# Spreading out the passage between the attention and the first expert stage: ten units of expert 0, one group's token sums, the Sinkhorn steps

## The chip, the cores and the metric

The kernel runs on one core of one Trainium2 chip. The engines of that core work at the same time, each through its own queue in order: TensorE (PE in the profile, with PEld for its weight loads), VectorE (DVE), ScalarE (ACT), GpSimd (POOL) and SyncE (SP, which here only issues transfers). The metric is the device time of one launch in microseconds (us), lower is better.

## What is computed

```python
# attention: r, k, v are [4, 8, 768, 48]; w, u are [8, 48]
for t in range(S):
    cur = einsum('bhd,bhe->bhde', u * k[t], v[t])
    y[t] = einsum('bhd,bhde->bhe', r[t], state + cur)
    state = w * state + einsum('bhd,bhe->bhde', k[t], v[t])
x = y.transpose(0, 2, 1, 3).reshape(3072, 384)
# eight experts over all 3072 tokens, with a Sinkhorn gate
P = exp(x @ w_gate - max)                  # [3072, 8]
for _ in range(8):
    P /= P.sum(1, keepdims=True) + 1e-09   # over the experts
    P /= P.sum(0, keepdims=True) + 1e-09   # over the tokens
    P *= N / E
out = sum over e of P[:, e:e+1] * (relu(x @ w1[e]) @ w2[e])   # w1 [8, 384, 1024], w2 [8, 1024, 384]
```

## The kernel before

**Attention.** The 3072 tokens are 24 tiles of 128. A loop over `i` (0 to 26) carries each tile through stages `prep`, `stage_b` to `stage_f`, one tile per pass and each stage one or more passes behind the one before it. At its end a tile stands in `hbx` as x transposed, in two float16 parts (high, and what is left), and its gate logits in `logits`. Three tiles make a position `po_` (384 tokens); there are eight.

**Expert 0** is computed plainly, in *units*. `g1_unit(po_, fc, W)` forms 128 hidden columns of one position: nine products of 128x384 into the PSUM tile `ph` (pool `ps1`, two banks), then a relu on ACT into `hb` (high part) and a scalar_tensor_tensor on DVE (low part, which needs the high one). `g2_half(po_, t, j, W)` is half of the second layer for one tile: twelve products into `po` (pool `ps2`, two banks), a copy on ACT into `stg`, and a store to `e0d` in DRAM by the SP queue. 109 units are made; `run` places three of them in each pass of the attention from `i` = 5 on, which leaves 43 units and the last three halves of the second layer (`pend`).

**Experts 1 to 7** are 14 stages of half an expert. Their first layer uses a scheme with 15 products in place of 18: the 384 inputs of a half's weights are combined into 15 weight sums, the tokens into 15 token sums. The token sums come in four groups `sg` of 768 tokens: `combine_tokens` gives `rebuild` (three DVE additions of the two parts of x), `singles` (four copies by transfers on the SP queue), `pool` (17 additions on POOL), and `high` and `low` in four pieces (`PARTS`): a cast on ACT and a difference on DVE into `xv`. Groups 0 and 1 (into `xv0`) are made in the attention, one step at each call of `prepare`; groups 2 and 3 (into `xv1`) after it. `stage_weights` does the like for weights: `load` into `rawb`, four `amax` on DVE, the maximum over the partitions (`reduce_max`, `across`, `scale`: two tiny products on PE with DVE work between them), 11 additions on POOL into `ucb`, eight pieces of `high` (ACT) and `low` (DVE) into `ws0` or `ws1`.

**The tick loop** lies between the attention and stage 0, and its order is written out by hand. Each tick does what `at(t, ...)` lists for it and then issues one unit of expert 0. It holds group 2, the first stage's weights `W0`, group 3, and the Sinkhorn: a generator `sk` of 21 steps, of which 16 are half steps (`rs` is the half over experts, on DVE alone; `cs` the half over tokens, a product `pc` on PE and then DVE). From tick 4 on a half step stands at every second tick, to tick 36.

**Stage s** is a row of *slots*. `g1_slots(s, g, j)` gives 15 slots of three products 128x512 each (tiles `bA`, `bY`, `bZ`, `bC`, `bB`, with DVE and ACT sums after most slots); `g` is the half of the tokens, `j` the half of the columns. Between the slots 24 products per five slots are taken from `rest`: in the first half of stage 0 (`g` = 0, 30 slots) that is `e0_rest`, the 36 products of `pend`; from then on it is `g2_tiles`, 144 products for the second layer of the group before. The stage's `at(t, ...)` puts weight work of the next stage at slots. A bank for a first-layer tile is taken from `ps4` (four banks), every third one from `ps1`. `gate()` and `gate0()` form the weights by which the second layer's results are scaled, from the finished gate `pm`.

All instructions carry line 29, where a helper records them; so they are told apart by their tiles.

Of the kernel before, what the change touches and what calls it, by code (L numbers as in the profile page):

```python
# [32 lines left out]
def rwkv_sinkhorn_moe(  # L33
# [175 lines left out]
    def g1_unit(po_, fc, W):  # L209
        w1h, w1l = W[0], W[1]  # L210
        hh, hl = h0(fc // FHC)
        ph = ps1.tile([P, TB], F32, tag="ph", name=f"ph_{po_}_{fc}")[:, :TB0]
        fs = slice(fc * P, (fc + 1) * P)
        for c in range(KC):
            xh_, xl_ = xx8[:, po_, c], xx8[:, po_, KC + c]
            T.matmul(ph, w1h[:, c, fs], xh_, start=(c == 0), stop=False)
            T.matmul(ph, w1h[:, c, fs], xl_, start=False, stop=False)
            T.matmul(ph, w1l[:, c, fs], xh_, start=False, stop=(c == KC - 1))
        fl = fc % FHC
        S_.activation(hh[:, fl, :], ph, AF.Relu)  # L220
        V.scalar_tensor_tensor(
            hl[:, fl, :], ph, 0.0, hh[:, fl, :], op0=ALU.max, op1=ALU.subtract
        )
# [450 lines left out]
    def token_steps(sg, *homes):  # L674

        rebuild, singles, pool, high, low = combine_tokens(sg, *homes)
        steps = [[lambda th=th: rebuild(th)] for th in range(TH)]
        steps[-1].append(singles)
        steps += [[f] for f in pool] + [[], [], [], []]
# [14 lines left out]
    def run(n, ready=True):  # L694
        prepare()
        if not ready:
            spin(5)
            return
        for _ in range(n):
            if units:  # L700
                units.pop(0)()

    W, side = split_weights(0, *raws, ws1)
    for sg in range(2):
        steps = token_steps(sg, ws0, 0, ws0, 9 * TS)
        need[id(steps[0])] = (sg + 1) * 2 * TH
        side += steps
# [4 lines left out]
    for i in range(NTT + 3):  # L712
# [28 lines left out]
        if 3 <= i < 8:  # L741
            prepare()
# [3 lines left out]
        if 0 <= done < NTT and done % TH == TH - 1:  # L746
            po_ = done // TH
            for j in range(2):
                g1 = [lambda fc=fc, po_=po_: g1_unit(po_, fc, W) for fc in range(j * FHC, (j + 1) * FHC)]
                g2 = [lambda a=a: whole(g2_half(*a, W)) for a in pend]  # L750
# [137 lines left out]
    WS = {0: stage_weights(0)}  # L888
    sk = sinkhorn()
    at(0, WS[0]["load"])  # L890
    for j in range(4):
        at(j, lambda: next(sk, None))
    for j in range(8):
        at(4 * j + 4, lambda: next(sk, None))
        at(4 * j + 6, lambda: next(sk, None))
    at(36, lambda: next(sk, None))

    def plan_tokens(sg, t_build, t_pool, pool_rate, t_parts, homes):
        rebuild, singles, pool, high, low = combine_tokens(sg, *homes)
        for th, t in enumerate(t_build):  # L900
            at(t, lambda th=th: rebuild(th))
        at(t_build[-1], singles)
        for i, f in enumerate(pool):
            at(t_pool + i // pool_rate, f)
        for (i, n), t in zip(((0, 3), (3, 3), (6, 3), (9, 4)), t_parts):
# [3 lines left out]
    plan_tokens(2, (0, 1, 2), 3, 3, (5, 7, 8, 10), (ucb, 0, tb_, 0))  # L909
    W0 = WS[0]  # L910
    for i, t in enumerate((4, 5, 9, 10)):
        at(t, lambda i=i: W0["amax"](i))
    at(11, W0["reduce_max"])
    at(12, W0["across"])
    for i, f in enumerate(W0["pool"]):
        at(9 + i // 3, f)
    at(14, W0["scale"])
    for n, i in enumerate((0, 1, 2, 3, 4, 5, 6, 7)):
        at(15 + n, lambda i=i: W0["high"](i))
        at(16 + n, lambda i=i: W0["low"](i))  # L920
    plan_tokens(3, (20, 20, 21), 21, 3, (24, 26, 27, 29), (ucb, 0, tb_, 0))

    tick = 0
    while units or any(t >= tick for t in ticks):
        for f in ticks.pop(tick, []):
            f()
        if units:
            units.pop(0)()
# [12 lines left out]
    def bank(name):  # L941
        n = chains[0]
        chains[0] += 1
        if n % 3 == 2:
# [152 lines left out]
    def stage_tasks(s):  # L1097
# [8 lines left out]
        at(2, gate)  # L1106
        if s == 0:
            at(3, gate0)
# [28 lines left out]
    def e0_rest():  # L1137
        for a_ in pend:
# [50 lines left out]
```

## Time and profile before

| | |
|---|---|
| three timed runs | 1598.94 us median (1598.56 to 1601.12) |
| the profiled execution, its own time | 1598.68 us |
| its span, first to last instruction | 1597.0 us |
| PE busy | 1567.8 us, 98% of the span |
| DVE, ACT, POOL busy | 1021.9, 668.0, 586.6 us |

Times in views are counted from the span's start. In a timeline row stand the start, the length, the engine, the line, the operation with its tiles, how many instructions the row merges, and in brackets the idle time of the engine ahead of it with what ended it. A row of the view by windows gives, for one stretch, its length, then busy time and instructions of PE, PEld, DVE, ACT and POOL, the granted PE clock as a share, the share of the transfer engines and GB/s. In the chain of work that ended last the rows are start, length, engine and tile; a product's length there is the time until the next one, without its drain, and so gives PE's rate.

### The profile page before, as it was taken

Reading aid. Unit: us, or ns where it says so; the run is one execution under the profiler, and the core shown is the slowest. Engines: PE = TensorE matmul, PEld = TensorE weight load, DVE = VectorE, ACT = ScalarE, POOL = GpSimd, SP = SyncE. Lnnn points to the kernel's source line nnn. Section 1 sums busy time; section 2 is a strip of 40 time slices with the busy share of each in tenths; the row PEclk is TensorE's granted clock in tenths of the full one; section 3 lists DMA queues with packets and bytes.
Section 4 is the critical chain, followed back from the end, with each engine's and each line's share of the span. In section 5 each row is a group of like instructions: output and inputs, shape, how many; then the busy total and the mean of one; then the engine's idle time right before and its main releaser. Section 6 shows DMA issues by size and latency. Waiting matters only on the chain.

```text
span 1597.0 us, 24269 instructions
## 1 busy us (share of the span) xinstructions
PE 1567.8 (98%) x9394; PEld 907.6 (57%) x9394; DVE 1021.9 (64%) x1693; ACT 668.0 (42%) x1190; POOL 586.6 (37%) x688
## 2 busy tenths in 40 slices
PE   7999999989999999999999999999999999999999
PEld 4777777655455555555555555555555555555555
DVE  6766766675766676666667666666666666656554
ACT  2333333343444444454535454544444453535420
POOL 6557665452020342424242424243242424242200
PEclk9999999999999999999999999999999999999999
DMA  7323330212122566666665666665555555555443
GB/s 179 64 65 77 78 87 26 89 44 84 34 95 58 104 88 115 88 124 87 122 95 86 113 88 120 89 115 62 94 58 95 60 97 59 95 59 89 60 93 129
DMA packets 167643, 138.32 MB, mean 87 GB/s; under 512 B 90337, under 2 KB 161762, under 8 KB 167522
## 3 DMA queue, kind: packets, MB, share of 16 engines
q0 software_dynamic: 44928, 61.36, 31.9%
q1 hardware_dynamic: 122384, 75.35, 16.9%
q8 instruction: 75, 1.23, 0.3%
q14 instruction: 46, 0.38, 0.1%
q10 hardware_dynamic: 210, 0.00, 0.0%
HBM read 55.39 MB, written 80.23 MB: 85 GB/s over the span
## 4 chain that ended last, share of the span: by engine, by line
PE 93%; DVE 3%; POOL 1%; issue 1%; ACT 1%; DMA 0%; ACTq 0%; DVEq 0%; POOLq 0%
PE po L29 46%; PE bY L29 11%; PE bZ L29 11%; PE ph L29 5%; PE bA L29 4%; PE bB L29 4%; PE py L29 4%; PE bC L29 2%; PE pA L29 1%; PE pu L29 1%; POOL tb L29 1%; PE prT L29 1%; PE pz L29 1%; PE pkT L29 1%; PE px L29 0%
## 5 line engine op out<-in xcount | busy, mean ns | idle before, releaser
L29 PE MATMUL po<-ws,hbx 128*128 128x384 f16 x3360 | 737.3, 327 | 0.0
L29 POOL DMA_DIRECT2D accd<-stg x288 | 249.8, 867 | 695.4 <-ACT stg L29 675.5
L29 PEld LDWEIGHTS <-hbx 128*128 128x128 f16 x3576 | 338.0, 98 | 291.4
L29 PEld LDWEIGHTS <-ws 128*128 128x128 f16 x3096 | 303.1, 98 | 251.9 <-issue 10.2
L29 ACT ACTIVATE hbx<-tb 128x512 f16<-128x512 f32 x224 | 141.0, 630 | 445.6 <-DVE tb L29 445.6
L29 PE MATMUL po<-ws,hb 128*128 128x384 f16 x1248 | 323.4, 328 | 3.2 <-DVE ws L29 2.3
L29 DVE TENSOR_TENSOR tb<-bY,tb 128x512 f32<-128x512 f32 x168 | 116.1, 691 | 195.3 <-PE bY L29 195.1
L29 ACT ACTIVATE stg<-po,pe 128x384 f32<-128x384 f32 x312 | 179.1, 574 | 121.8 <-PE po L29 94.9
L29 PE MATMUL bZ<-xv,ws 128*128 128x512 f16 x840 | 227.8, 381 | 1.4 <-DVE tb L29 1.4
L29 PE MATMUL bY<-xv,ws 128*128 128x512 f16 x840 | 227.8, 381 | 1.1 <-DVE tb L29 1.1
L29 DVE TENSOR_TENSOR tb<-bZ,tb 128x512 f32<-128x512 f32 x168 | 115.4, 687 | 134.2 <-PE bZ L29 134.2
L29 PEld LDWEIGHTS <-hb 128*128 128x128 f16 x1248 | 122.1, 98 | 96.5 <-issue 5.0
L29 POOL TENSOR_TENSOR ucb<-rawb 128x256 f32<-128x256 f32 x84 | 75.0, 943 | 94.8 <-DMA rawb<-in_moe_w_dram 68.3
L29 DVE TENSOR_TENSOR tb<-bB,tb 128x512 f32<-128x512 f32 x112 | 77.4, 691 | 48.9 <-PE bB L29 47.0
L29 PE MATMUL ph<-hbx,ws 128*128 128x384 f16 x576 | 103.8, 329 | 1.2 <-DVE hb L29 1.2
L29 DVE SCALAR_TENSOR_TENSOR hb<-tb,hbx 128x512 f16<-128x512 f32 x112 | 77.3, 690 | 24.6 <-ACT hbx L29 19.5
L29 PE MATMUL bA<-xv,ws 128*128 128x512 f16 x336 | 90.9, 380 | 1.0 <-ACT tb L29 1.0
L29 PE MATMUL bB<-xv,ws 128*128 128x512 f16 x336 | 90.9, 380 | 0.0
L29 DVE SCALAR_TENSOR_TENSOR hbx<-tb,hbx 128x512 f16<-128x512 f32 x112 | 78.2, 698 | 14.7 <-ACT hbx L29 10.4
L29 DVE SCALAR_TENSOR_TENSOR hb<-ph,hb 128x384 f16<-128x384 f32 x64 | 35.5, 555 | 58.9 <-ACT hb L29 58.8
L29 ACT COPY tb<-bZ 128x512 f32<-128x512 f32 x56 | 32.8, 585 | 67.6 <-PE bZ L29 67.6
L29 ACT ACTIVATE hb<-ph 128x384 f16<-128x384 f32 x64 | 31.4, 491 | 58.0 <-PE ph L29 56.7
(165 smaller groups left out, 1638.3 us busy)
## 6 DMA issues: line engine op xcount, KB each, us to landing
accd<-stg POOLq DMA_DIRECT2D x288, 192.0 KB, 3.7
rawb<-in_moe_w_dram SPq DMA_DIRECT2D x28, 768.0 KB, 7.3
e0d<-stg SPq DMA_DIRECT2D x48, 192.0 KB, 1.9
hb<-e0d SPq DMA_DIRECT2D x48, 192.0 KB, 3.7
rn<-in_r_dram SPq DMA_DIRECT2D x24, 192.0 KB, 3.1
kn<-in_k_dram SPq DMA_DIRECT2D x24, 192.0 KB, 3.6
vn<-in_v_dram SPq DMA_DIRECT2D x24, 192.0 KB, 2.7
accd<-stg SPq DMA_DIRECT2D x24, 192.0 KB, 1.8
```

Source lines behind the costliest of these rows:

```text
L29: return lambda *a, **k: self.tc.keep_in_program_order(f(*a, **k))
```

## The change

Five things, all between the last passes of the attention and the end of the first half of stage 0.

1. Expert 0's last ten units (six `g1_unit`, four `g2_half`) are taken off the tick loop, which keeps 33. They go ahead of `pend` in `e0_rest`, so that 138 products (102 and 36) are there for the 144 places between the 30 slots. For this `g1_unit` becomes a generator that stops after each product.
2. Group 2's `rebuild` and its 17 POOL additions become steps of the attention (`token_steps(..., sums=True)`), in `ws0` and not in `ucb` and `tb`. `prepare` is called once or twice more in a pass from `i` = 21. Its casts and differences stay in the tick loop, at ticks 0 to 7, its `singles` go from tick 2 to 0.
3. Group 3 comes ahead of the weights: `rebuild` at ticks 0 to 2, `singles` at 2, casts at 8 to 14 (before: 20 and 21, 21, 24 to 29). `W0`'s `across` and `scale` go from ticks 12 and 14 to 14 and 17, its `high` and `low` from 15 to 23 to 18 to 26.
4. The Sinkhorn's half steps stand two or three ticks apart (4, 7, 9, 12, ... 32), and the last five steps at slots 2, 5, 9, 13 and 18 of stage 0. `gate` and `gate0` of that stage move from slots 2 and 3 to 24 and 25.
5. The first ten banks of the first layer all come from `ps4`, since `ph` of the moved units uses `ps1`.

```diff
@@ -207,6 +207,7 @@
         return (part(hb3, F16, 2 * j * n, (FHC, TB0)), part(hb3, F16, (2 * j + 1) * n, (FHC, TB0)))
 
     def g1_unit(po_, fc, W):
+
         w1h, w1l = W[0], W[1]
         hh, hl = h0(fc // FHC)
         ph = ps1.tile([P, TB], F32, tag="ph", name=f"ph_{po_}_{fc}")[:, :TB0]
@@ -214,13 +215,17 @@
         for c in range(KC):
             xh_, xl_ = xx8[:, po_, c], xx8[:, po_, KC + c]
             T.matmul(ph, w1h[:, c, fs], xh_, start=(c == 0), stop=False)
+            yield
             T.matmul(ph, w1h[:, c, fs], xl_, start=False, stop=False)
+            yield
             T.matmul(ph, w1l[:, c, fs], xh_, start=False, stop=(c == KC - 1))
-        fl = fc % FHC
-        S_.activation(hh[:, fl, :], ph, AF.Relu)
-        V.scalar_tensor_tensor(
-            hl[:, fl, :], ph, 0.0, hh[:, fl, :], op0=ALU.max, op1=ALU.subtract
-        )
+            if c == KC - 1:
+                fl = fc % FHC
+                S_.activation(hh[:, fl, :], ph, AF.Relu)
+                V.scalar_tensor_tensor(
+                    hl[:, fl, :], ph, 0.0, hh[:, fl, :], op0=ALU.max, op1=ALU.subtract
+                )
+            yield
 
     def g2_half(po_, t, j, W):
 
@@ -671,12 +676,15 @@
 
     PARTS = ((0, 3), (3, 3), (6, 3), (9, 4))
 
-    def token_steps(sg, *homes):
-
-        rebuild, singles, pool, high, low = combine_tokens(sg, *homes)
+    def token_steps(parts, sums=False):
+
+        rebuild, singles, pool, high, low = parts
         steps = [[lambda th=th: rebuild(th)] for th in range(TH)]
-        steps[-1].append(singles)
-        steps += [[f] for f in pool] + [[], [], [], []]
+        steps += [[f] for f in pool]
+        if sums:
+            return [lambda fs=fs: [f() for f in fs] for fs in steps]
+        steps[2].append(singles)
+        steps += [[], [], [], []]
         for (i, n), at_ in zip(PARTS, (5, 11, 15, 19)):
             steps[TH + at_].append(lambda i=i, n=n: high(i, n))
             steps[TH + at_ + 1].append(lambda i=i, n=n: low(i, n))
@@ -698,11 +706,12 @@
             return
         for _ in range(n):
             if units:
-                units.pop(0)()
+                whole(units.pop(0))
 
     W, side = split_weights(0, *raws, ws1)
-    for sg in range(2):
-        steps = token_steps(sg, ws0, 0, ws0, 9 * TS)
+    early = [combine_tokens(sg, ws0, 0, ws0, 9 * TS) for sg in range(3)]
+    for sg in range(3):
+        steps = token_steps(early[sg], sg == 2)
         need[id(steps[0])] = (sg + 1) * 2 * TH
         side += steps
     prep(0)
@@ -738,7 +747,9 @@
         if 1 <= i <= NTT:
             stage_d(i - 1)
         prepare()
-        if 3 <= i < 8:
+        if 3 <= i < 8 or i >= 21:
+            prepare()
+        if i >= 22:
             prepare()
         if 3 <= i:
             stage_f(i - 3)
@@ -746,8 +757,8 @@
         if 0 <= done < NTT and done % TH == TH - 1:
             po_ = done // TH
             for j in range(2):
-                g1 = [lambda fc=fc, po_=po_: g1_unit(po_, fc, W) for fc in range(j * FHC, (j + 1) * FHC)]
-                g2 = [lambda a=a: whole(g2_half(*a, W)) for a in pend]
+                g1 = [g1_unit(po_, fc, W) for fc in range(j * FHC, (j + 1) * FHC)]
+                g2 = [g2_half(*a, W) for a in pend]
                 units += merged(g1, g2)
                 pend = [(po_, t, j) for t in range(TH)]
     assert not side
@@ -885,47 +896,49 @@
     def at(t, *fs):
         ticks.setdefault(t, []).extend(fs)
 
-    WS = {0: stage_weights(0)}
-    sk = sinkhorn()
-    at(0, WS[0]["load"])
-    for j in range(4):
-        at(j, lambda: next(sk, None))
-    for j in range(8):
-        at(4 * j + 4, lambda: next(sk, None))
-        at(4 * j + 6, lambda: next(sk, None))
-    at(36, lambda: next(sk, None))
-
-    def plan_tokens(sg, t_build, t_pool, pool_rate, t_parts, homes):
-        rebuild, singles, pool, high, low = combine_tokens(sg, *homes)
-        for th, t in enumerate(t_build):
-            at(t, lambda th=th: rebuild(th))
-        at(t_build[-1], singles)
-        for i, f in enumerate(pool):
-            at(t_pool + i // pool_rate, f)
-        for (i, n), t in zip(((0, 3), (3, 3), (6, 3), (9, 4)), t_parts):
+    def at_parts(high, low, t_parts):
+        for (i, n), t in zip(PARTS, t_parts):
             at(t, lambda i=i, n=n: high(i, n))
             at(t + 1, lambda i=i, n=n: low(i, n))
 
-    plan_tokens(2, (0, 1, 2), 3, 3, (5, 7, 8, 10), (ucb, 0, tb_, 0))
-    W0 = WS[0]
-    for i, t in enumerate((4, 5, 9, 10)):
+    W0 = stage_weights(0)
+    WS = {0: W0}
+    sk = sinkhorn()
+    at(0, W0["load"])
+    for t in (0, 1, 2, 3, 4, 7, 9, 12, 14, 17, 19, 22, 24, 27, 29, 32):
+        at(t, lambda: next(sk, None))
+
+    _, singles2, _, high2, low2 = early[2]
+    at(0, singles2)
+    at_parts(high2, low2, (0, 2, 4, 6))
+
+    rebuild3, singles3, pool3, high3, low3 = combine_tokens(3, ucb, 0, tb_, 0)
+    for th in range(TH):
+        at(th, lambda th=th: rebuild3(th))
+    at(2, singles3)
+    for i, f in enumerate(pool3):
+        at(2 + i // 2, f)
+    at_parts(high3, low3, (8, 10, 12, 14))
+
+    for i, t in enumerate((5, 8, 9, 11)):
         at(t, lambda i=i: W0["amax"](i))
     at(11, W0["reduce_max"])
-    at(12, W0["across"])
+    at(14, W0["across"])
     for i, f in enumerate(W0["pool"]):
-        at(9 + i // 3, f)
-    at(14, W0["scale"])
-    for n, i in enumerate((0, 1, 2, 3, 4, 5, 6, 7)):
-        at(15 + n, lambda i=i: W0["high"](i))
-        at(16 + n, lambda i=i: W0["low"](i))
-    plan_tokens(3, (20, 20, 21), 21, 3, (24, 26, 27, 29), (ucb, 0, tb_, 0))
-
+        at(11 + i // 2, f)
+    at(17, W0["scale"])
+    for i in range(W0["n"]):
+        at(18 + i, lambda i=i: W0["high"](i))
+        at(19 + i, lambda i=i: W0["low"](i))
+
+    e0_last = units[-10:]
+    del units[-10:]
     tick = 0
     while units or any(t >= tick for t in ticks):
         for f in ticks.pop(tick, []):
             f()
         if units:
-            units.pop(0)()
+            whole(units.pop(0))
         tick += 1
 
 
@@ -941,7 +954,7 @@
     def bank(name):
         n = chains[0]
         chains[0] += 1
-        if n % 3 == 2:
+        if n % 3 == 2 and n >= 10:
             return ps1.tile([P, TB], F32, tag="ph", name=name)
         return ps4.tile([P, TB], F32, tag="pq", name=name)
 
@@ -1103,9 +1116,11 @@
         def gate():
             pes[s] = gate_of(1 + s // 2, WS[s]["isw"], s)
 
-        at(2, gate)
+        at(2 if s else 24, gate)
         if s == 0:
-            at(3, gate0)
+            at(25, gate0)
+            for t in (2, 5, 9, 13, 18):
+                at(t, lambda: next(sk, None))
         if s + 1 < NS:
             w_ = WS[s + 1] = stage_weights(s + 1)
             at(0, w_["load"])
@@ -1135,6 +1150,8 @@
         return ts
 
     def e0_rest():
+        for u_ in e0_last:
+            yield from u_
         for a_ in pend:
             yield from g2_half(*a_, W)
 
```

Three places show what moves. The first is **POOL at the end of the attention**: `rk` is the attention's last work there, `tb<-ucb` are token sums after it, `ws_74` is `ws0`. Before:

```order
L29 TENSOR_TENSOR rk_6445<-rk_6445,hbx 128x384
L29 TENSOR_TENSOR S_6625<-S_6625,wbd 128x384
L29 TENSOR_TENSOR rk_6571<-vn_6187,dg_6710 128x384
L29 TENSOR_TENSOR rk_6571<-rk_6571,hbx 128x384
L29 TENSOR_TENSOR tb<-ucb 128x256 x4
L29 TENSOR_TENSOR tb<-tb,ucb 128x256 x2
```

Now:

```order
L29 TENSOR_TENSOR rk_6445<-rk_6445,hbx 128x384
L29 TENSOR_TENSOR S_6625<-S_6625,wbd 128x384
L29 TENSOR_TENSOR rk_6571<-vn_6187,dg_6713 128x384
L29 TENSOR_TENSOR rk_6571<-rk_6571,hbx 128x384
L29 TENSOR_TENSOR ws_74<-ws_74 128x256 x17
L29 TENSOR_TENSOR tb<-ucb 128x256 x4
```

Group 2's 17 additions follow the attention's last POOL work; the sums into `tb` behind them are now group 3's. No unit of PE and no attention product changes its place up to here.

The second is **DVE ahead of `wmas`**, the result of `reduce_max` for which PE's `across` product waits. `xv` is `low`, `wms` is `amax`, `hb` a unit's low part. Before:

```order
L29 TENSOR_TENSOR xv_6996<-tb,xv_6996 128x3x256
L29 SCALAR_TENSOR_TENSOR hb_73<-ph_4_7175,hb_73 128x384
L29 TENSOR_TENSOR xv_6996<-tb,xv_6996 128x3x256
L29 TENSOR_REDUCE wms_7003<-rawb 128x1
L29 TENSOR_REDUCE cs_7210<-pc_7208 128x8
L29 TENSOR_SCALAR cs_7210<-cs_7210 128x8
L29 RECIPROCAL cs_7210<-cs_7210 128x8
L29 TENSOR_TENSOR pm<-pm,cs_7210 128x192
L29 TENSOR_REDUCE wms_7003<-rawb 128x1
L29 SCALAR_TENSOR_TENSOR hb_73<-ph_5_7220,hb_73 128x384
L29 TENSOR_TENSOR xv_6996<-tb,xv_6996 128x4x256
L29 TENSOR_REDUCE wmas_7004<-wms_7003 128x2
```

Now:

```order
L29 TENSOR_TENSOR xv_7016<-tb,xv_7016 128x3x256
L29 TENSOR_REDUCE wms_7023<-rawb 128x1
L29 SCALAR_TENSOR_TENSOR hb_73<-ph_5_7234,hb_73 128x384
L29 TENSOR_TENSOR xv_7016<-tb,xv_7016 128x3x256
L29 TENSOR_REDUCE wms_7023<-rawb 128x1
L29 TENSOR_REDUCE wmas_7024<-wms_7023 128x2
L29 TENSOR_REDUCE cs_7269<-pc_7267 128x8
L29 TENSOR_SCALAR cs_7269<-cs_7269 128x8
L29 RECIPROCAL cs_7269<-cs_7269 128x8
L29 TENSOR_TENSOR pm<-pm,cs_7269 128x192
L29 SCALAR_TENSOR_TENSOR hb_73<-ph_6_7277,hb_73 128x384
L29 TENSOR_TENSOR xv_7016<-tb,xv_7016 128x3x256
```

In the last piece before `wmas` the half step `cs` now stands behind it, and the differences around it are group 3's, with group 2's already done; `wmas` is emitted at tick 11 as before, the product that waits for it at tick 14, not 12.

The third is **PE at the turn from `j` = 0 to `j` = 1 in the first half of stage 0**. Three products stand under each name, of which one is shown, with LDWEIGHTS between them. Before:

```order
L29 MATMUL bB_0_0_7913<-xv_76,ws_74 128x512
L29 LDWEIGHTS ws_74
L29 MATMUL bA_0_1_7952<-xv_76,ws_74 128x512
...
L29 LDWEIGHTS ws_74
L29 MATMUL bY_0_1_7962<-xv_76,ws_74 128x512
```

Now:

```order
L29 MATMUL bB_0_0_7770<-xv_76,ws_74 128x512
...
L29 LDWEIGHTS hb_73
L29 MATMUL po_0_7823<-ws_75,hb_73 128x384
...
L29 LDWEIGHTS ws_74
L29 MATMUL bA_0_1_7859<-xv_76,ws_74 128x512
...
L29 LDWEIGHTS ws_75
L29 MATMUL ph_6_7869<-hbx,ws_75 128x384
...
L29 LDWEIGHTS ws_74
L29 MATMUL bY_0_1_7875<-xv_76,ws_74 128x512
```

Where slot followed slot, four or five products of expert 0's units (`po`, `ph`) now lie between two slots.

## The prediction

> **What bounds the kernel now.** I first read the view by windows, to see where PE (98% busy) is not full.
>
> ```profile
> 280.00:320.00 40.00, 37.44 (x263) 24.14 (x261) 25.91 (x53) 14.32 (x28) 17.50 (x22) 1.00 0.29 92
> 320.00:360.00 40.00, 36.20 (x208) 21.42 (x209) 31.15 (x67) 16.32 (x28) 20.48 (x24) 0.96 0.13 42
> 360.00:400.00 40.00, 38.23 (x215) 20.89 (x213) 20.69 (x41) 13.37 (x26) 8.79 (x12) 1.00 0.25 84
> 400.00:440.00 40.00, 37.07 (x183) 18.14 (x182) 30.08 (x48) 19.92 (x34) 0.00 (x0) 0.96 0.13 34
> 440.00:480.00 40.00, 40.00 (x220) 21.38 (x219) 26.22 (x38) 16.64 (x30) 8.44 (x11) 1.00 0.28 94
> 600.00:800.00 200.00, 200.00 (x1095) 106.90 (x1094) 131.44 (x200) 96.83 (x171) 72.19 (x87) 1.00 0.66 107
> ```
>
> From 440 us on PE has no gap and the full clock (1.00): there PE is the bound, and the change adds and removes no product. Between 280 and 440 us 11.06 us of PE are idle (40 less each PE column), and the clock falls to 0.96 twice. Then I read PE's timeline through that stretch: its first tick, the gaps over half a microsecond, and the first product of the second half of stage 0.
>
> ```profile
> 296.05 1.62 PE L29 MATMUL ph<-hbx,ws 128*128 128x384 f16 x9
> 320.69 0.27 PE L29 MATMUL pmax_s<-ident,wmas 128*2 128x128 f32 x1 [3.23 <-DVE wmas L29]
> 320.80 2.27 PE L29 MATMUL ph<-hbx,ws 128*128 128x384 f16 x9
> 326.66 0.59 PE L29 MATMUL pc<-pm,ones 128*128 128x192 f32 x2 [0.61 <-ACT stg L29]
> 350.33 0.56 PE L29 MATMUL pc<-pm,ones 128*128 128x192 f32 x2 [2.02 <-DVE pm L29]
> 362.61 2.11 PE L29 MATMUL po<-ws,hb 128*128 128x384 f16 x12 [0.92 <-DVE cs L29]
> 397.14 0.81 PE L29 MATMUL bZ<-xv,ws 128*128 128x512 f16 x3 [0.66 <-DVE tb L29]
> 401.65 0.81 PE L29 MATMUL bA<-xv,ws 128*128 128x512 f16 x3 [1.04 <-ACT tb L29]
> 403.57 1.44 PE L29 MATMUL bY<-xv,ws 128*128 128x512 f16 x3 [1.11 <-DVE tb L29]
> 410.57 0.81 PE L29 MATMUL bZ<-xv,ws 128*128 128x512 f16 x3 [0.58 <-DVE tb L29]
> 413.60 0.81 PE L29 MATMUL bA<-xv,ws 128*128 128x512 f16 x3
> ```
>
> All gaps stand between 296.05 and 413.60 us, and almost all end with DVE: the weights' maximum, the Sinkhorn, the first layer's sums. After the 3.23 us gap nine products take 2.27 us, where the first row has 1.62; after the pair 1.04 and 1.11, three take 1.44 in place of 0.81: PE also comes back slow.
>
> What would this stretch last without gaps? The chain of waits gives PE's rates, length until the next product.
>
> ```profile
> 320.69 0.27 PE pmax_s L29
> 327.26 0.31 PE pmax_s L29 x2
> 334.01 0.33 PE pc L29 x2
> 368.86 2.92 PE ph L29 x18
> 371.78 1.95 PE po L29 x12
> 382.02 0.65 PE bA L29 x3
> 382.67 0.81 PE po L29 x5
> ```
>
> 25 units `ph` (2.92 / 2 = 1.46 each) are 36.5 us, 18 units `po` 35.1, the 36 products of `pend` (0.81 / 5 = 0.163) 5.9, 30 slots of 0.65 19.5, eight `pc` 2.6, and two `pmax` pairs of 0.11 (320.69 to 320.80) and 0.31 0.8: 100.4 us. The stretch is 413.60 - 296.05 = 117.55 us. So **17.1 us is the most that can go**: 11 us of gaps, the rest slow products and drains.
>
> **The change part by part.** *The order of units.* The same 25 + 18 units and 36 products are issued; ten units move behind the first slots. That costs nothing by itself, and covers slots 8 to 29, which stood bare. With 138 products the first half of stage 0 lasts 19.5 + 138 x 0.163 + two `pc` 0.7 = 42.7 us on PE, the tick loop 57.7. In the bare slots a product had to wait for sums of the slots just before; now 1.46 us (0.65 + 0.81) go by from slot to slot and not 0.65.
>
> *Sums into the attention.* 17 POOL additions and three DVE additions move ahead of 296 us.
>
> ```profile
> 274.30:296.05 21.75, 21.75 (x185) 15.80 (x183) 8.00 (x21) 6.25 (x14) 0.02 (x1) 1.00 0.10 37
> 301.72 2.78 POOL L29 TENSOR_TENSOR tb<-ucb 128x256 f32<-128x256 f32 x4 [27.40 <-PE po L29]
> 312.90 3.53 POOL L29 TENSOR_TENSOR tb<-tb,ucb 128x256 f32<-128x256 f32 x3
> 316.46 1.04 ACT L29 CAST xv<-tb 128x1024 f16<-128x1024 f32 x1 [2.17 <-POOL tb L29]
> ```
>
> The same 17 took 301.72 to 316.43 = 14.7 us. POOL is free for 21.7 us from 274.30, so they end near 289, and DVE is 37% busy there (8.00 of 21.75): cost 0. Past 296 us POOL would hold up the first transfers and writes into the memory that the attention frees; a miss of 7 us is needed for that. At 316.46 ACT waited 2.17 us for these sums, and the relus, `wmas` and PE waited behind it. Group 3's sums, from about 302 to 318, now feed casts at ticks 8 to 14, which PE's pace puts at 310 to 321: no wait expected. The eight `singles` on SP come ahead of stores, whose buffers are wanted only at tick 9: 0.
>
> *DVE in the first 18 ticks.* This decides how much comes back.
>
> ```profile
> 296.05:334.17 38.12, 34.26 (x204) 20.27 (x200) 28.38 (x62) 14.72 (x27) 22.77 (x28) 0.96 0.28 88
> L29 DVE TENSOR_TENSOR xv<-tb,xv 128x768 f16<-128x768 f32 x6 | 7.8, 1302 | 0.0
> L29 DVE TENSOR_TENSOR xv<-tb,xv 128x1024 f16<-128x1024 f32 x2 | 2.4, 1220 | 0.0
> L29 DVE SCALAR_TENSOR_TENSOR ws<-ucb,sw,ws 128x768 f16<-128x768 f32 x3 | 3.0, 1012 | 0.0
> 311.34 0.34 DVE L29 TENSOR_REDUCE rs<-pm 128x24 f32<-128x192 f32 x1
> 312.95 1.48 DVE L29 TENSOR_TENSOR xv<-tb,xv 128x768 f16<-128x768 f32 x1
> ```
>
> These ticks held 28.4 us of DVE (the third busy figure, after PE and PEld). They gain group 3's four differences (3 x 1.30 + 1.22 = 5.1), lose one half step (312.95 - 311.34 = 1.6) and two weight pieces (2.0): 29.9 us. PE needs, for the 11 `ph` and 7 `po` units of these ticks, 11 x 1.46 + 7 x 1.95 + three `pc` 1.0 + the `pmax` pairs 0.8 = 31.5. DVE is 95% booked, about as in the old order, but PE asks later: `across` three ticks after `wmas` and not one, each `pc` two or three ticks (3.4 to 5.4 us) after its `rs`. Laying the new DVE order against PE's pace with these lengths, `wmas` ends some 0.7 us ahead of `across`, and only a low part needed at tick 16 is late, by 0.4 us; I bound this term by 0 and 3.2 (the old gap). The 0.61 us at 326.66 stays: that `pc` still finds one `po` bank held by `across` and must wait for the copy of the unit just before it. Ticks 18 to 32 are light.
>
> *DVE at the turn of the slots.*
>
> ```profile
> L29 DVE SCALAR_TENSOR_TENSOR hb<-ph,hb 128x384 f16<-128x384 f32 x25 | 13.8, 553 | 21.4 <-ACT hb L29 21.4
> L29 DVE TENSOR_REDUCE wms<-rawb 128x1 f32<-128x768 f32 x8 | 7.4, 940 | 0.0
> L29 DVE SCALAR_TENSOR_TENSOR hbx<-tb,hbx 128x512 f16<-128x512 f32 x7 | 5.2, 739 | 1.1 <-ACT hbx L29 0.7
> L29 DVE TENSOR_TENSOR tb<-bZ,tb 128x512 f32<-128x512 f32 x6 | 4.1, 682 | 1.0 <-PE bZ L29 1.0
> ```
>
> Slots 9 to 14 now hold two half steps (some 2.8), three `amax` (2.8), three sums (2.1), three low parts (2.2) and one of a unit (0.55): 10.5 us of DVE in about 8.8 of PE, so DVE falls behind by 2 to 4 us just where, with four banks and no others, a product follows closely on the reader of its bank. I expect 0.5 us at slot 13 and another 0.5 at the turn; bounds 0 and 5.2 (the old gaps there, 3.6, and the slow products after 403.57, 1.6).
>
> On slow PE after a gap, the rows say 3.23 us, or two gaps of 1 us, bring it. The Trainium skill ("TensorE: Matmul & The Clock Gate", Part 1) says that the clock halves after an idle window of about 3.4 us; by it short gaps at the turn would cost no clock, by row 403.57 up to 1.6 us, and the measured row decides.
>
> **Sum:** 1598.7 (this execution; the median of the runs is 0.3 above) - 17.1 + 0.6 + 0.4 + 1.0 = **1583.6 us**.
>
> **The rivals.** *(1) DVE and POOL slow each other more.* `xv` took 1.48 us at 312.95 with POOL at work, and
>
> ```profile
> 257.77 0.94 DVE L29 TENSOR_TENSOR xv<-ws,xv 128x768 f16<-128x768 f32 x1
> ```
>
> without much of it. With all eight differences at 1.48 in a stretch where POOL now runs without a break from 302 to about 326 us, DVE gets 8 x 0.2 = 1.6 more: 31.5, as much as PE's 31.5, and then every wait of DVE for a relu delays PE; I price that at 3 us: 1586.6. The Trainium skill ("SBUF — State Buffer", Who interferes with whom) states such a rule, DVE with two SBUF inputs blocked for the whole POOL instruction; the 1.48 against 0.94 agrees with it.
>
> *(2) The turn of the slots keeps its gaps:* four banks and a late DVE bring back the 5.2 us: 1583.6 - 1.0 + 5.2 = 1587.8. For it speaks the count above; against it, that waits at slots 0 to 7 are covered by twice the PE work.
>
> *(3) The tick loop gains nothing,* DVE being 95% booked: then only the bare slots' 5.2 us and half of the drains go, about 1593. Against it: the waits named in the rows were asked one or two ticks after their DVE work, and now three.
>
> *(4) Slower.* DVE, in order, becomes the bound through the six units' low parts inside the slots: each waits for a relu, that for a product, that for a bank which DVE frees. DVE's gaps (117.55 less 82.21 busy in this row) would stay,
>
> ```profile
> 296.05:413.60 117.55, 106.48 (x596) 59.24 (x593) 82.21 (x162) 43.48 (x80) 46.77 (x56) 0.97 0.23 70
> 382.58 0.56 DVE L29 SCALAR_TENSOR_TENSOR hb<-ph,hb 128x384 f16<-128x384 f32 x1 [2.85 <-ACT hb L29]
> ```
>
> and six waits grow from 0.86 (21.4 / 25) to 2.85: + 12 us, less the 2.8 of the moved additions: 1608. It decides once DVE is over two `ph` units, 2.9 us, late for good. Against it: DVE waits for relus when it is early, not when it is late.
>
> **How the numbers follow.** Forecast 0.70; (1) 0.13, (2) 0.10, (3) 0.04, (4) 0.03. The forecast's own range is 1581.6 (no stall at all) to 1586. For 8 in 10 I take 1581 to 1590, which leaves out (3), (4) and the ends of (2). A change of under 0.2% (3.2 us) can't be told from none; faster by more has 0.95 (all but (4) and a tail of (3)), the same 0.02, slower 0.03.
>
> **What would show it.** In the new profile: POOL busy from about 274 to 290 us; no row of `pmax` or `pc` with over 1 us of idle ahead of it, but the 0.6 at one `pc`; the first `bA` of stage 0 near 355 us, that of its second half near 398.5 and not 413.6; clock 1.00 in all windows from 300 us; the rest moved whole, 15 us earlier. Wrong would be a gap ahead of `across` (rival 1 or 3), gaps with a slow clock between 365 and 375 us (2), or PE waits inside the attention, which I expect unchanged.

## The result, and the profile after

| | before | after |
|---|---|---|
| runs shown first, median (range) | 1599.31 us (1598.56 to 1601.12, 4 runs) | 1585.38 us (1581.19 to 1586.59, 4 runs) |
| ratio of the times, 95% interval | | 0.9907 (0.9892 to 0.9923) |
| profiled execution, its own time and span | 1598.68, 1597.0 us | 1586.59, 1584.9 us |
| first unit of the tick loop starts at | 296.05 us | 298.94 us |
| tick loop, to the first `bA` of stage 0 | 85.81 us | 59.35 us |
| first half of stage 0, to the first `bA` of the second | 31.74 us | 43.21 us |
| both together | 117.55 us | 102.56 us |
| from there to the end of the span | 1183.4 us | 1183.4 us |

The changed kernel is 0.9% faster, as forecast; 1583.6 us was predicted, inside the range of the runs and 1.8 us under their median. This is the view by windows of the changed kernel (columns as before: length, PE, PEld, DVE, ACT, POOL, granted clock).

```profile
280.00:320.00 40.00, 39.98 (x280) 25.86 (x278) 26.83 (x54) 16.56 (x31) 24.15 (x31) 1.00 0.31 93
320.00:360.00 40.00, 39.32 (x240) 23.66 (x239) 29.57 (x68) 18.91 (x33) 11.05 (x13) 1.00 0.13 46
360.00:400.00 40.00, 39.56 (x217) 21.37 (x216) 29.98 (x58) 12.71 (x26) 8.22 (x11) 1.00 0.21 72
400.00:440.00 40.00, 40.00 (x220) 21.31 (x219) 27.44 (x43) 21.25 (x37) 0.00 (x0) 1.00 0.16 60
298.94:330.50 31.56, 30.86 (x193) 18.48 (x189) 29.76 (x54) 15.52 (x27) 24.33 (x28) 1.00 0.37 112
```

Between 280 and 440 us PE is idle for 1.14 us, where it was 11.06, and the clock is full throughout. The last row covers the first 18 ticks: DVE is busy for 29.76 of 31.56 us. Now PE's timeline of the changed kernel: the loop's start, what stands around the two gaps that are left, and the second half of stage 0.

```profile
298.94 1.62 PE L29 MATMUL ph<-hbx,ws 128*128 128x384 f16 x9
...
323.66 0.27 PE L29 MATMUL pmax_s<-ident,wmas 128*2 128x128 f32 x1
323.77 3.09 PE L29 MATMUL ph<-hbx,ws 128*128 128x384 f16 x18
326.69 2.35 PE L29 MATMUL po<-ws,hb 128*128 128x384 f16 x12
329.66 0.59 PE L29 MATMUL pc<-pm,ones 128*128 128x192 f32 x2 [0.61 <-ACT stg L29]
...
358.29 0.81 PE L29 MATMUL bA<-xv,ws 128*128 128x512 f16 x3
...
377.98 0.81 PE L29 MATMUL bZ<-xv,ws 128*128 128x512 f16 x3 [0.44 <-DVE tb L29]
...
401.50 0.81 PE L29 MATMUL bA<-xv,ws 128*128 128x512 f16 x3
```

The 3.23 us ahead of `pmax_s` are gone, and so is the slow clock behind them. From loop start to the second half of stage 0 the kernel gained 117.55 - 102.56 = 15.0 us. But the loop started 2.89 us later. The place is an old gap far ahead of everything that the change touches: the two rows before are from the timeline and the windows of the kernel before, the next two from the changed one.

```profile
85.56 1.27 PE L29 MATMUL po<-ws,hb 128*128 128x384 f16 x5 [2.29 <-DVE ws L29]
84.00:104.00 20.00, 18.44 (x147) 15.14 (x147) 12.19 (x25) 4.55 (x10) 10.55 (x10) 0.91 0.23 52
```

```profile
85.71 1.11 PE L29 MATMUL po<-ws,hb 128*128 128x384 f16 x5 [2.29 <-DVE ws L29]
84.00:104.00 20.00, 18.29 (x118) 14.92 (x117) 10.23 (x19) 4.36 (x9) 9.30 (x8) 0.74 0.18 40
```

Both kernels wait the same 2.29 us for the split of expert 0's second weights. After it the clock averaged 0.91 over 20 us in one and 0.74 in the other: (0.91 - 0.74) x 20 = 3.4 us, which is the late start and a little more. Whether the change does this, or chance, was the first question.

### The profile page after: what moved, and what is told of

Same layout as the page of the kernel before. It is cut to its first block, busy times and chain, and to the rows that moved or that the text cites. A ratio compares the mean times of both kernels' runs of the same rounds, so it can differ in the third digit from the quotient of the medians.

```text
span 1584.9 us, 24259 instructions
## 1 busy us (share of the span) xinstructions
PE 1565.7 (99%) x9394; PEld 909.5 (57%) x9394; DVE 1021.0 (64%) x1693; ACT 667.7 (42%) x1190; POOL 585.1 (37%) x688
## 4 chain that ended last, share of the span: by engine, by line
PE 95%; DVE 3%; ACT 1%; issue 0%; ACTq 0%; DVEq 0%
PE po L29 47%; PE bZ L29 11%; PE bY L29 11%; PE ph L29 5%; PE bA L29 5%; PE bB L29 5%; PE py L29 4%; PE bC L29 2%; PE pA L29 1%; PE pu L29 1%; PE prT L29 1%; PE pz L29 1%; PE pkT L29 1%; PE px L29 0%; DVE xv L29 0%
## 5 line engine op out<-in xcount | busy, mean ns | idle before, releaser
L29 ACT ACTIVATE xsc<-x,xs 128x384 f32<-128x384 f32 x24 | 14.8, 616 | 97.5 <-DVE xs L29 88.1
```

The lines of the kernel that those rows point to most:

```text
L29: return lambda *a, **k: self.tc.keep_in_program_order(f(*a, **k))
```

## The experiments

All were measured beside the kernel before on the same chip. The three middle columns are taken from PE's timeline of each profile, between the same products as above; the clock is that of the window from 84 to 104 us.

| run | loop starts | tick loop | stage 0, first half | both | clock, 84 to 104 us | median of runs (range), ratio and interval |
|---|---|---|---|---|---|---|
| before | 296.05 | 85.81 | 31.74 | 117.55 | 0.91 | |
| after | 298.94 | 59.35 | 43.21 | 102.56 | 0.74 | 1585.38 (1581.19 to 1586.59), 0.9907 (0.9892 to 0.9923) |
| again | 298.15 | 59.34 | 43.16 | 102.50 | 0.74 | 1584.38 (1581.13 to 1585.83), 0.9916 (0.9902 to 0.9929) |
| units | 294.57 | 68.54 | 42.17 | 110.71 | 0.91 | 1592.50 (1589.81 to 1595.20), 0.9971 (0.9961 to 0.9980) |
| nounits | 297.60 | 76.57 | 31.90 | 108.47 | 0.74 | 1587.04 (1586.03 to 1591.17), 0.9937 (0.9922 to 0.9952) |
| oldtok | 298.82 | 64.25 | 43.08 | 107.33 | 0.74 | 1589.02 (1586.93 to 1591.26), 0.9936 (0.9919 to 0.9953) |
| oldsink | 297.97 | 60.52 | 42.17 | 102.69 | 0.74 | 1582.73 (1581.18 to 1585.75), 0.9898 (0.9881 to 0.9914) |
| oldbank | 293.45 | 59.36 | 48.70 | 108.06 | 1.00 | 1586.61 (one run) |
| nosums3 | 297.95 | 59.06 | 43.08 | 102.14 | 0.74 | 1585.20 (one run) |
| early | 291.84 | 59.34 | 43.42 | 102.76 | 1.00 | 1579.24 (1578.97 to 1579.69), 0.9890 (0.9875 to 0.9905) |
| skew | 292.79 | 58.46 | 43.47 | 101.93 | 1.00 | 1578.53 (1577.82 to 1579.83), 0.9868 (0.9852 to 0.9885) |
| best | 288.81 | 58.47 | 43.28 | 101.75 | 1.00 | 1576.14 (1575.66 to 1576.46), 0.9856 (0.9839 to 0.9872) |

The whole times scatter by 4 to 6 us with the early clock; "both" repeats within 0.1 us (102.56 and 102.50 for the same kernel). So the parts of the change are judged by that column. Each row is one profile, though, and where a gap of over 3 us is left in the stretch, the clock behind it is chance there too (see "oldtok").

### Once more: again

The changed kernel, unedited.

> The changed kernel once more, unedited. In its first profile the first unit of the tick loop starts at 298.94 us, 2.89 us later than before the change, because the clock stayed low up to 97 us after the 2.29 us gap at 85.7 us, and only up to 91 us before the change. My theory: how long the clock stays low after that gap is chance. Then the tick loop starts anywhere from 294 to 299 us from one execution to the next, the runs lie between 1581 and 1587 us with the higher mean clock in the shorter ones, and from the loop's first unit to the first product of the second half of stage 0 it takes 102.3 to 102.9 us each time (102.56 in the first profile). The rival: the change itself lengthens the attention; then the loop starts at 298.5 us or later again and no run is under 1583 us.

The runs lie between 1581.13 and 1585.83 us, and "both" is 102.50. This profile had the low clock again (298.15 us); but an edited kernel with exactly the changed kernel's attention (oldbank) started its loop at 293.45. And at the same clock of 0.74 the old attention (oldtok) starts the loop at 298.82 us, the new one at 297.60 to 298.94. So the rival, that the change lengthens the attention, falls: the window behind the gap averaged 1.00, 0.91 or 0.74, and nothing between, and it did so with the old attention (before 0.91, units 0.91, oldtok 0.74) and with the new (oldbank 1.00, the rest 0.74). Here is that window for oldbank, which has the same gap.

```profile
84.62 0.97 PE L29 MATMUL po<-ws,hb 128*128 128x384 f16 x5 [2.28 <-DVE ws L29]
84.00:104.00 20.00, 19.38 (x173) 15.61 (x172) 13.82 (x27) 6.12 (x13) 10.92 (x9) 1.00 0.35 79
```

### The gap at 85 us taken away: early

```diff
             for j in range(2):
 ...
+                if j and not po_:
+                    units.append(g1.pop(0))
                 units += merged(g1, g2)
```

> One thing is added to the change: in position 0 the first unit of the second half of the hidden columns is not followed by a half of the second layer but by the next unit, so that the first po comes one ph unit (1.46 us) and some attention work later, behind the second part of the split weights that it waited for. Theory, the gap brings the low clock: the 2.29 us at 85.7 us go, and the low clock from 86 to 91 or 97 us (2 to 5 us lost) goes with them; 1577 to 1580 us, runs within 2 us of each other, the tick loop starting near 291 to 293 us. Rival, the low clock at this place has another cause (the kind of work, the transfers): only the gap goes, 1582 to 1583 us, and the clock between 85 and 97 us still falls under 0.8. A second rival, the wait moves to the next product: no gain, 1585 us.

The gap is gone, and this is the window in its place:

```profile
84.00:104.00 20.00, 19.96 (x176) 15.74 (x175) 16.43 (x31) 5.47 (x12) 11.55 (x11) 1.00 0.36 79
```

The clock is full, the loop starts at 291.84 us, and four runs lie within 0.7 us of each other, where the changed kernel's lie 5 us apart. 1579.24 us is inside what the theory gave (1577 to 1580); the rivals' 1582 and 1585 are out. So the low clock at this place hangs on the gap; "skew" and "best", which leave it out too, also have 1.00 there.

### The units alone, and all but the units: units and nounits

In "units" the token sums and the first weights keep their old ticks, and so does the Sinkhorn up to tick 32; only the ten units move, with the new rule for the banks:

```diff
-    for t in (0, 1, 2, 3, 4, 7, 9, 12, 14, 17, 19, 22, 24, 27, 29, 32):
+    for t in (0, 1, 2, 3, *range(4, 33, 2)):
 ...
+    plan_tokens(2, (0, 1, 2), 3, 3, (5, 7, 8, 10), (ucb, 0, tb_, 0))
 ...
+    plan_tokens(3, (20, 20, 21), 21, 3, (24, 26, 27, 29), (ucb, 0, tb_, 0))
 ...
-            for t in (2, 5, 9, 13, 18):
+            for t in (2, 5):
```

> Only the ten units are moved (with the new rule for the banks); the token sums, the first weights and the Sinkhorn stand at their old ticks, and the two Sinkhorn steps that no longer fit the shorter loop are at slots 2 and 5, the gates at 24 and 25. Theory: the slots are covered (43 us for 42.6 of products), but the loop of 33 units keeps the old gaps of 3.23, 0.61, 2.02, 0.48 and 0.92 and the slow products behind them, 57.8 + 10 = 68; together 111 and about 1594 us. Rival, the move of the units brings all: 103, 1586 us. Rival, the extra units between the slots cost as much as they cover, since DVE is late there: 117, 1599 us.

Expected were 68 and 43, 111 in all; measured 68.54 and 42.17, 110.71. The gaps stand where the theory put them, as PE's timeline of "units" shows:

```profile
319.22 0.27 PE L29 MATMUL pmax_s<-ident,wmas 128*2 128x128 f32 x1 [3.24 <-DVE wmas L29]
325.20 0.59 PE L29 MATMUL pc<-pm,ones 128*128 128x192 f32 x2 [0.61 <-ACT stg L29]
348.87 0.56 PE L29 MATMUL pc<-pm,ones 128*128 128x192 f32 x2 [2.03 <-DVE pm L29]
356.26 0.56 PE L29 MATMUL pc<-pm,ones 128*128 128x192 f32 x2 [0.49 <-DVE pm L29]
361.16 2.11 PE L29 MATMUL po<-ws,hb 128*128 128x384 f16 x12 [0.93 <-DVE cs L29]
```

"nounits" is the reverse:

```diff
-    e0_last = units[-10:]
-    del units[-10:]
+    e0_last = []
 ...
-    for t in (0, 1, 2, 3, 4, 7, 9, 12, 14, 17, 19, 22, 24, 27, 29, 32):
+    for t in (0, 1, 2, 3, 4, 7, 9, 12, 14, 17, 19, 22, 24, 27, 29, 32, 34, 37, 39, 42, 42):
 ...
-        if n % 3 == 2 and n >= 10:
+        if n % 3 == 2:
```

> The ten units stay in the tick loop (43 units, the old rule for the banks), the last five Sinkhorn steps go to ticks 34 to 42 and the gates back to slots 2 and 3; the sums in the attention, the new order of the ticks and the spread half steps stay. Theory: the tick loop loses its gaps by the order of DVE alone: 25 x 1.46 + 18 x 1.95 + 8 x 0.33 + 0.8 = 75.0 and some 1.5 of rest, 76.5 us where it was 85.8; the bare slots keep their old length, 31.7; together 108.2 and not 102.6, about 1591 us. Rival, the move of the units brings all: the loop stays near 84 to 86, 1599 us. Rival, DVE is the bound of the loop: 80 or more.

Expected were 76.5 and 31.7; measured 76.57 and 31.90. The loop has only the 0.61 us gap; stage 0 has the old ones, slow products behind them included:

```profile
328.31 0.59 PE L29 MATMUL pc<-pm,ones 128*128 128x192 f32 x2 [0.61 <-ACT stg L29]
389.62 0.81 PE L29 MATMUL bZ<-xv,ws 128*128 128x512 f16 x3 [0.84 <-DVE tb L29]
394.14 0.81 PE L29 MATMUL bA<-xv,ws 128*128 128x512 f16 x3 [1.04 <-ACT tb L29]
396.06 1.44 PE L29 MATMUL bY<-xv,ws 128*128 128x512 f16 x3 [1.11 <-DVE tb L29]
```

So of the 15.0 us the moved units bring 117.55 - 110.71 = 6.8 alone and the order of the loop 117.55 - 108.47 = 9.1 alone; together nearly all of their sum. (Its median of 1587 lies under the 1591 expected; the profiled run, with the clock at 0.74, took 1591.17.)

### The sums back behind the attention: oldtok

The ticks of both token groups and of the first weights as in "units", the Sinkhorn spread as in the change.

> The sums of group 2 go back behind the attention, and the token groups, the first weights and their maximum to their old ticks; the moved units, the spread Sinkhorn and the banks stay as changed. Theory: the 3.23 us ahead of the first pmax_s product, the slow products behind it (1.8) and the 0.61 return, the three pc gaps (2.02, 0.48, 0.92) do not: the loop of 33 units takes 57.8 + 5.9 = 63.7 us (59.35 with the change), stage 0's first half 43.2 as with the change; 106.9 and 4.3 us longer than the change. Rival, the gaps come from DVE's whole amount and not from the late sums: all stay, 68.5. Rival, the old pc gaps return as well, because they hang on the light parts of the weights: over 66.

64.25 and 43.08, 107.33 in all, against 63.7, 43.2 and 106.9: the size is right, but by luck, since only some of its pieces came. PE's gaps in the loop, and the window behind the first:

```profile
323.89 0.27 PE L29 MATMUL pmax_s<-ident,wmas 128*2 128x128 f32 x1 [3.66 <-DVE wmas L29]
358.49 0.34 PE L29 MATMUL po<-ws,hb 128*128 128x384 f16 x1 [1.21 <-DVE hb L29]
361.12 2.11 PE L29 MATMUL po<-ws,hb 128*128 128x384 f16 x12 [0.48 <-ACT stg L29]
323.89:328.00 4.11, 4.11 (x26) 2.47 (x27) 3.45 (x12) 0.84 (x2) 4.11 (x7) 1.00 0.00 0
```

The gap ahead of `pmax_s` returns (3.66). The 0.61 does not, and neither do the slow products behind the gap, for which 1.8 us were expected: the clock there is full, where in "before" it averaged 0.61 from 320.69 to 325 us. In their place 1.21 and 0.48 stand late in the loop, where group 3's differences are. Early sums and the order they allow are worth 107.33 - 102.56 = 4.8 us in these two profiles. With the clock of "before" behind the gap it would be some (1 - 0.61) x 4.31 = 1.7 us more, by my estimate.

### The Sinkhorn at every second tick: oldsink

```diff
-    for t in (0, 1, 2, 3, 4, 7, 9, 12, 14, 17, 19, 22, 24, 27, 29, 32):
+    for t in (0, 1, 2, 3, *range(4, 33, 2)):
 ...
-            for t in (2, 5, 9, 13, 18):
+            for t in (2, 5):
```

> The half steps of the Sinkhorn go back to every second tick from 4 to 32 (two of the last steps stay at slots 2 and 5); all else as changed. Theory: group 2's maximum is in time, so no 3.23; but DVE gets 1.6 us more in the first 18 ticks, where it is 94% busy, and each pc is asked two ticks after its rs: the gaps of 2.02, 0.48 and 0.92 return, and some more ahead of tick 18; the loop 59.35 + 3.4 = 62.8 to 65 us, stage 0's first half 42.2 (fewer steps in the slots). Rival, the pc gaps came from the old place of the weights' low parts and go without the spreading too: 60 us or less.

My theory is wrong here: 60.52 us in the loop and not 62.8 to 65. Only the two half steps that fall into the full first 18 ticks make PE wait:

```profile
316.37 0.59 PE L29 MATMUL pc<-pm,ones 128*128 128x192 f32 x2 [0.73 <-DVE pm L29]
324.57 0.56 PE L29 MATMUL pc<-pm,ones 128*128 128x192 f32 x2 [0.78 <-DVE pm L29]
```

The old gaps of 2.02, 0.48 and 0.92 stay away without the spreading. "units" has this Sinkhorn with the old ticks of the token groups and the first weights, and has them; so they came from half steps that stand close while that work lies beside them. No run separates which part of that work it is. In "units" DVE is busy for 11.10 of the 11.41 us ahead of the 2.03 us gap (337.31 to 348.72), with group 3's three additions of `rebuild` and four low parts of the weights among the half steps; group 3's differences follow only behind that gap, ahead of the next two. And since "oldsink" leaves fewer steps between the slots, its first half of stage 0 has no gap at all (42.17): both together 102.69 against 102.56. The spreading is worth 0.1 us.

### The banks by the old rule: oldbank

```diff
-        if n % 3 == 2 and n >= 10:
+        if n % 3 == 2:
```

> The first ten banks of the first layer follow the old rule again (every third from ps1), so the moved ph units have one bank of ps1 for long stretches. Theory: where two ph units follow each other between the slots, the second waits for relu and low part of the first: two or three gaps of 0.5 to 2 us, stage 0's first half 45 to 47 us where it was 43.2; the loop unchanged, 59.3. Rival, the slot products between two units hide it: 43.2 to 43.6, and the new rule for the banks is worth nothing.

Worse than expected: 48.70 us, 5.5 more than with the new rule.

```profile
366.34 1.44 PE L29 MATMUL ph<-hbx,ws 128*128 128x384 f16 x4 [3.64 <-DVE hb L29]
367.57 1.48 PE L29 MATMUL bY<-xv,ws 128*128 128x512 f16 x3
...
381.73 0.97 PE L29 MATMUL ph<-hbx,ws 128*128 128x384 f16 x5 [0.59 <-DVE hbx L29]
```

A `ph` unit behind another waits 3.64 us for the one bank left to it (until DVE has written the low part of the unit ahead), and the clock is low behind it: three `bY` products take 1.48 us and not 0.81.

### Group 3's sums left out: nosums3

```diff
-    for i, f in enumerate(pool3):
-        at(2 + i // 2, f)
+    at(2, lambda: G.memset(tb_[:, : 13 * TS], 0.0))
```

> The 17 additions of POOL for group 3 are left out; one POOL instruction fills their results with zeros (those tokens' sums are then zero). If POOL slows DVE, the four xv differences of group 3 fall from 1.34 and 1.36 us to about 0.95 and 1.2, the three of group 2 from 1.12 to 0.95, and DVE has 2 us less in the loop; the loop of 59.35 us loses at most 0.3 to 0.5, since the 0.61 gap hangs on a bank and not on DVE. Rival, the lengths go with the tile and not with POOL: they stay, and the loop too. If the loop falls by over 1 us, DVE was the bound of it after all.

DVE's differences from 290 to 337 us, first of the changed kernel, then of this one (count, then busy us and mean ns):

```profile
L29 DVE TENSOR_TENSOR xv<-tb,xv 128x768 f16<-128x768 f32 x3 | 4.0, 1340 | 0.0
L29 DVE TENSOR_TENSOR xv<-ws,xv 128x768 f16<-128x768 f32 x3 | 3.3, 1116 | 0.0
```

```profile
L29 DVE TENSOR_TENSOR xv<-tb,xv 128x768 f16<-128x768 f32 x3 | 2.8, 948 | 0.0
L29 DVE TENSOR_TENSOR xv<-ws,xv 128x768 f16<-128x768 f32 x3 | 3.4, 1118 | 0.0
```

With POOL's additions gone, group 3's differences take 0.95 us and not 1.34, as expected. Group 2's were expected to fall too, and do not. The first two take 0.94 in both kernels. The third takes 1.48 in both, beside group 3's additions in the changed kernel and here beside additions for the first weights, which POOL now takes up at 304.94 us already:

```profile
306.47 1.57 POOL L29 TENSOR_TENSOR ucb<-ucb,rawb 128x256 f32<-128x256 f32 x2
307.38 1.48 DVE L29 TENSOR_TENSOR xv<-ws,xv 128x768 f16<-128x768 f32 x1
```

The loop falls by 0.3 us, at the lower end of the forecast: POOL does slow DVE, and PE hardly waits for it. Nearly all of the 0.3 is one row: the twelve `po` products that take 2.35 us at 326.69 in the changed kernel take 2.11 here.

### A better version: skew and best

"skew" takes the unit order of "early", moves one half step behind the `scale` that frees a bank, and keeps slots 9 to 14 free of Sinkhorn steps; "best" also gives one maximum its bank elsewhere.

```diff
-    for t in (0, 1, 2, 3, 4, 7, 9, 12, 14, 17, 19, 22, 24, 27, 29, 32):
+    for t in (0, 1, 2, 3, 4, 7, 9, 12, 14, 18, 20, 22, 24, 26, 28, 30, 32):
 ...
-            for t in (2, 5, 9, 13, 18):
+            for t in (2, 4, 7, 16):
```

> On top of the unit order of the run called early: the half step of tick 17 goes to 18, behind the scale that frees a po bank, the later ones stand at every second tick to 32, and the four last Sinkhorn steps at slots 2, 4, 7 and 16, so that slots 9 to 14 hold none. Theory: the 0.61 gap goes (it hangs on the bank held by pmax_s), one more pc (0.33) stands in the loop; 58.6 to 59.2 us and not 59.35; the 0.45 and 0.15 at the turn of the slots go, since DVE holds 2.8 us less there; stage 0's first half 42.2 to 42.5 and not 43.2 to 43.4; together about 101.2, near 1578 us. Rival, the copy of the unit ahead still ends later than the bank's release: the 0.61 stays, 59.8. Rival, the turn's gap comes from the maximum of the next weights alone: it stays, 43.

The loop has no gap left, 58.46 us; it holds six `pc` as in the changed kernel, and not one more as expected. The gap in slot 13, ahead of the turn, goes, but a new one comes in slot 11:

```profile
368.61 0.81 PE L29 MATMUL bZ<-xv,ws 128*128 128x512 f16 x3 [0.81 <-DVE tb L29]
```

DVE comes to the half step of slot 7 only at 366.31 us, and the sum over `bZ` that ends this gap follows behind it, at 367.88. So the first half of stage 0 stays at 43.47, and the forecast of 42.2 to 42.5 was wrong. That the gap goes with the half step is borne out by "oldsink" and "units", whose last steps stand at slots 2 and 5: they have no gap between the slots.

```diff
-                res[j] = over_partitions(ma_[j], 1, ps1, "ph", f"w{e}_{j}")
+                res[j] = over_partitions(ma_[j], 1, (ps1, ps2)[j], ("ph", "po")[j], f"w{e}_{j}")
```

> The run called skew, and the product pmax_w of the second weight matrix of expert 0 takes its bank from ps2 and not from ps1, where it left one bank for two ph units. Theory: the 1.17 us ahead of the ph product near 70 us go, the tick loop starts 1.0 to 1.5 us earlier (290.5 and not 291.8), about 1577 us. Rival, another wait takes its place within the same pass of the attention, since the products there hang on DVE: the start stays near 291.8, 1578 us.

The loop starts at 288.81 us, 3.0 earlier than in "early". Half of this is older: the first `pu` product with a wait stands at 47.26 us in "early" and at 45.71 in "best". From there to the loop it is 244.58 and 243.10 us, 1.5 less, at the upper end of what was expected for the 1.17 us gap. ("skew", with the attention of "early", took 245.24 us for this piece; but its clock averaged 0.80 from 60 to 65 us, where the other two have 1.00.) These are that product and the next waits of "best"; none follows near 70 us.

```profile
45.71 1.13 PE L29 MATMUL pu<-vn,kp 128*128 128x96 f32 x8 [0.67 <-ACT rT L29]
54.18 1.16 PE L29 MATMUL pA<-rT,kT 64*128 64x128 f32 x14 [0.36 <-ACT rT L29]
58.58 1.13 PE L29 MATMUL py<-S,rT 128*128 128x96 f32 x8 [0.77 <-DVE at L29]
63.32 0.27 PE L29 MATMUL pmax_w<-ident,wma 128*1 128x128 f32 x1 [0.73 <-DVE wma L29]
```

"best" took 1576.14 us, 0.9856 (0.9839 to 0.9872) of the kernel before, whose interval lies wholly under that of the change.

## Why the prediction was right, and where it was wrong

**The bound and the most that can go.** Right: nothing behind the first half of stage 0 changed (1183.4 us in both), and the stretch had 117.55 - 100.4 us to give. 102.56 was measured where the sum had 100.4 + 0.6 + 0.4 + 1.0 = 102.4. The marks named, 355 and 398.5 us for the first `bA` of each half, came at 358.29 and 401.50: both late by the 2.9 us of the start, and by at most 0.4 more. That the sum came out to 0.2 us is partly luck, as two misses cancel: the tick loop took 59.35 us where 57.7 + 1.0 was forecast, 0.65 more, and the first half of stage 0 took 43.21 where 42.7 + 1.0 was, 0.5 less.

**The three stalls.** The bank at the `pc` of tick 17: 0.6 forecast, 0.61 measured, and gone in "skew", where that `pc` stands behind the `scale`. The late low part at tick 16: 0.4 forecast; the row at 326.69 has 2.35 us where others of its kind have 2.11, so 0.24 ("nosums3" has 2.11 there). The slots: 0.5 at slot 13 forecast and 0.44 measured; the other 0.5 did not come. Two second `pmax` products that wait for DVE, 0.19 us each by their starts, were not in the sum.

**The sums into the attention.** Right: POOL's 17 additions, one row of the changed kernel's timeline,

```profile
278.18 12.62 POOL L29 TENSOR_TENSOR ws<-ws 128x256 f32<-128x256 f32 x17
```

end at 290.80, 8.1 us ahead of the loop (7 were forecast), and PE is full there. "oldtok" gives their worth.

**DVE in the first 18 ticks.** 29.9 us of 31.5 forecast, 29.76 of 31.56 measured. Being 94% booked did not make it the bound: rivals 1 and 3 fall, the first with its mechanism shown and its price not (0.3 us of loop, and not 3).

**The Sinkhorn.** Wrong in its reason: I let the `pc` gaps go because "PE asks later". "oldsink" shows that asking two ticks behind is enough from tick 18 on, once the token groups and the first weights stand at their new ticks; and what the spreading saves in the loop it gives back among the slots, with the gap of 0.44 and one more `pc`.

**The units.** "That costs nothing by itself" holds only with the new rule for the banks, to which I gave no price: 5.5 us ("oldbank"). In the forecast that edit was mere accompaniment; it guards most of the 6.8 us that the units bring.

**The step that missed: what lies ahead of 296 us.** The sum was made against one execution, with everything before the loop taken as fixed ("the rest moved whole, 15 us earlier"). In that execution the gap at 85 us cost (1 - 0.91) x 20 = 1.8 us of clock; in the changed kernel's it cost 5.2. That is 3.4 us, of which 2.89 reached the loop's start; and 1598.68 + 2.89 - 15.0 is the 1586.6 that was measured, 3.0 us over the forecast. The rows for it were in the profile of before, but the prediction read the rows of PE only from 274 us on. No term of the sum or the range stood for this clock: that all runs lie between 1581 and 1590 us owes something to a range made wide for other reasons. Rival 2 and the slower rival found no support: the turn keeps 0.44 us, and DVE's waits for relus did not pass on to PE.

## What to carry to other kernels

Work out what a stretch would last without gaps, from the counts and the engine's own rates, and price a reordering against that: here each of the two pieces was right to 0.7 us and their sum, partly by luck, to 0.2, while the whole time scattered by 5 us. An order by hand pays where it moves a late producer or covers a bare stretch, not by spreading steps as such; and when work is put between other work, count the banks that both take. Look for gaps anywhere on the bounding engine, also far from the edit: here one of 2.3 us cost its length and then a clock that differed from run to run.

## What the runs showed of the hardware

Behind the same gap of about 2.3 us, the granted clock over the next 20 us averaged 1.00, 0.91 or 0.74, nothing else in the nine profiles that have the gap: a loss of 0, 1.8 or 5.2 us, in whole steps (one step of about 1.75, or three). The lowest rows show a clock of 0.50 for whole 5 us windows; this is the view by windows of "again" behind its gap:

```profile
85.00:90.00 5.00, 5.00 (x27) 4.72 (x26) 0.89 (x2) 0.96 (x2) 0.72 (x1) 0.59 0.00 0
90.00:95.00 5.00, 5.00 (x30) 4.08 (x30) 3.41 (x8) 1.57 (x3) 2.83 (x2) 0.50 0.43 103
95.00:100.00 5.00, 5.00 (x40) 3.32 (x38) 3.32 (x6) 0.49 (x1) 2.19 (x4) 0.89 0.28 58
```

A gap's length did not settle whether the clock fell. Gaps of 3.2 to 3.7 us inside the stretch brought it down in three of four profiles ("before", "units" and "oldbank", not "oldtok"), and 1.17 us near 70 us in none of eleven. Behind a gap of 0.8 us near 60 us it fell in four of twelve ("before", "after", "oldtok", "skew"). These are the windows of "before", where it fell, and of "again", where it did not:

```profile
60.00:65.00 5.00, 5.00 (x42) 4.76 (x43) 4.20 (x12) 0.00 (x0) 4.18 (x6) 0.72 0.17 34
60.00:65.00 5.00, 4.27 (x44) 3.93 (x45) 4.52 (x12) 0.10 (x1) 4.50 (x6) 1.00 0.21 43
```

From 60 to 70 us each of these four lost 1.7 us of clock, one step. That this short gap is the cause was not tested.

The Trainium skill ("TensorE: Matmul & The Clock Gate", Part 1) says that the clock is full or half, decided over free-running windows of about 3.4 us. The steps agree with it: by an estimate from that figure, one such window at half speed would lose 1.7 us, three 5.1. That an idle window is needed for the clock to fall, as the table there has it, is not borne out as it stands: 2.29 us of idle did it in eight of nine profiles. Why it is then one window in some executions and three in others stays open.
